# First rounds of an attention stage in a new order: second pair of keys loaded ahead of v, loads dealt out over the rounds

## The chip, the cores and the metric

The kernel runs on one core of a Trainium2 chip. The metric is the device time of one execution in microseconds (us); the median of three runs counts. A core has five engines with instruction queues of their own, each worked off in order: PE (TensorE, matrix products), DVE (VectorE), ACT (ScalarE), POOL (GpSimd) and SP (SyncE, which here only issues DMAs). PEld is PE's loading of stationary operands.

## The reference

Three stages in float32, one behind the other:

```python
# q, k, v: (2, 8, 576, 64)
q_d, k_d, v_d = means of q, k, v over 4 neighbouring positions        # 144 of them
out_d   = softmax(q_d k_d' / 8) v_d, each row repeated 4 times
out_loc = softmax(q k' / 8 where |i - j| < 4) v                       # a narrow band
x = out_d + out_loc                                                    # 1152 tokens x 512
h = x @ w_in;  x = (h * clip(h + 3, 0, 6) / 6) @ w_out                 # 512 -> 2048 -> 512
out = sum over 4 experts of p[e] * (relu(x @ w1[e]) @ w2[e])           # 512 -> 1024 -> 512
```

## The kernel before

Dense products are made in three passes over a high and a low part of each operand, so every weight is first converted (split in two) on ACT and DVE: the generator `converting()` takes one step whenever `convert(n)` asks for n of them. Six steps make one weight block (the first two blocks are called wt[0] and wt[1] here): ACT's top half (L221), DVE's L245, L255, L267 with L276, ACT's L229, and DVE's L234, which ends it.

The attention stage is the first tenth of the time. It works on eight **units** (a batch and a pair of heads; 0 to 3 are batch 0), one a round, in a loop over t (L1111 to L1176). A unit's steps on PE, with the line that the profile shows:

- `pooled_scores` (L726): scores of the pooled rows. It needs `sums`: sums over four positions of q and k, made on POOL (L450; of k on DVE, L636, in units 0 and 1) from what DMA has brought.
- `masks` and `scores` (L650, L663): the band's scores, over a mask.
- `turn` (L710) and `pooled_turn` (L780): transposes of the two softmaxes, after DVE, ACT and POOL have made them (`less_max`, `normalise`, `pooled_softmax`, `pooled_normalise`).
- `values` (L800, L811): products with v. ACT then copies the pooled part (pd, L819), DVE adds both (xf, L825), ACT and DVE split the sum (L833, L841). A unit is turned one round after its scores, its values come a round later.
- `idle_products` (L603): products of zeros whose result nobody reads.

Once per batch v is pooled: `pool_v` (L470, on PE) for batch 0; for batch 1 `pool_last_v` (L483, on PE, from v's last block of 67 rows) and `add_four(0)`, `add_four(1)` (L450 on DVE, from two loads of 512 KB that `load_four` issues at L500).

All engines but SP run in the order of the program text. PE's results go to three double banks in turn (`banks()`; a fourth, `banks(True)`, serves pool_v and values), so a step also waits until the step three banks back has been read. DMAs go through SP's queue; a load that must not start early is preceded by `hold`, a write of one element on DVE (L189), which SP waits for. The list `later` holds such loads; `load_next` takes the next one at three places of a round:

```python
    later = [
        lambda: load_half(0, 0),        # w_in, half a block
        lambda: load_half(0, 1),
        lambda: load_v(1, 0, (0,)),
        ...
        last_v,
        lambda: load_k(NU // 2 - 1, held=True),
        lambda: load_q(NU // 2 - 1, held=True),
        lambda: load_four(0),
        lambda: load_four(1),
        ...
```

From t = 8 on, `pieces(1)` puts the first products with w_in between the last units: the first (0, 0) needs wt[0], the third (0, 2) wt[1].

Of the kernel before, what the change touches and what calls it, by code (L numbers as in the profile page):

```python
# [25 lines left out]
ALU = mybir.AluOpType  # L26
AX = mybir.AxisListType
PSUM = bass.MemoryType.PSUM

P = 128  # L30
# [4 lines left out]
FACTOR = 4  # L35
# [80 lines left out]


IDLE = 11


def r32(ap):
# [4 lines left out]
def model(ctx: ExitStack, tc: tile.TileContext, qT, kT, v, dp, w_in, w_out, w1, w2, out):  # L126
# [284 lines left out]
    def load_qk(pair, at=0, n=2):  # L411
        load_k(pair, at, n)
        load_q(pair, at, n)
# [11 lines left out]
    def load_v(b, p, parts=(0, 1)):  # L425
        if 0 in parts:
            v_slots.setdefault(b, []).append(take())
        slot, o = v_slots[b][p][0], FACTOR - 1
        if b and p < 2:
            hold(slot[:, 2 * DM * parts[0] :])  # L430
        if p == 0:
            if 0 in parts:
                nc.vector.memset(slot[:o, :DM], 0.0)
                v_rows(b, p, o, 0, WR, 0, 1)
                v_rows(b, p, WP, WP - o, WP, 0, 1)
                v_rows(b, p, 0, QB - o, P, 1, 2)
# [16 lines left out]

        return v_slots[b][NP - 1][0][: KR[b][kc], (2 + kc) * DM : (3 + kc) * DM]

    def pool_v(idle):

        pool = banks(True)
        idle_products(pool, idle)
# [17 lines left out]
        for kc in range(2):  # L477
            nc.scalar.activation(out=pooled_v(0, kc), in_=pool[: KR[0][kc], kc, :], func=AF.Copy)
# [42 lines left out]
    nc.vector.memset(zeros, 0.0)  # L521
    load_qk(0, 0, 1)
    load_qk(0, 1, 1)
    for p in range(NP):
        load_v(0, p)
    load_qk(1)
    identb = const.tile([P, P], BF16, name="identb")
    make_identity(nc, identb)

# [68 lines left out]
            )  # L598
        nc.gpsimd.tensor_copy(fours[WP:], fours[:WP])

    def idle_products(ps, count):
        for n in range(count):
            nc.tensor.matmul(ps[:, n % 2, :], zeros[:, :P], zeros, start=True, stop=True)  # L603

    class Unit:
        def __init__(self, u):
# [1 line left out]
            self.b, self.hp = divmod(u, NHP)  # L608
            self.kr = KR[self.b]

        def sums(self):
# [8 lines left out]
            room = slice(2 * SK + 2 * PK, 2 * SK + 4 * PK)  # L620
            kr = KR[0]
            wide = slice(room.start, room.start + 4 * kr[0])
            own = self.k[:, FACTOR - 1 : FACTOR - 1 + S]
            k4 = k[:, base + FACTOR - 1 : base + FACTOR - 1 + NI * QT]
            k4 = k4.rearrange("p (a r j f) -> p r a j f", a=NI, r=2, f=FACTOR)
            k2 = k[:, wide].rearrange("p (a r j f) -> p r a j f", a=NI, r=2, f=2)
            if self.u >= 2:
                of = own.rearrange("p (j f) -> p j f", f=FACTOR)
                half = k[:, room].rearrange("p (j f) -> p j f", f=2)
                add(nc.gpsimd, half, of[:, :, 0:2], of[:, :, 2:4])  # L630
            if self.b:
                add(nc.gpsimd, self.kd, half[:, :, 0], half[:, :, 1])
            for r in range(0 if self.b else 2):
                to = self.kd[:, r * kr[0] : r * kr[0] + kr[r]].rearrange("p (a j) -> p a j", a=NI - r)
                if self.u < 2:
                    nc.vector.tensor_reduce(out=to, in_=k4[:, r, : NI - r], op=ALU.add, axis=AX.X)  # L636
                else:
                    two = k2[:, r, : NI - r]
                    add(nc.gpsimd, to, two[:, :, :, 0], two[:, :, :, 1])
            of = self.q.rearrange("p (j f) -> p j f", f=FACTOR)  # L640
            half = q[:, room].rearrange("p (j f) -> p j f", f=2)
            add(nc.gpsimd, half, of[:, :, 0:2], of[:, :, 2:4])
            add(nc.gpsimd, self.qd, half[:, :, 0], half[:, :, 1])

        def masks(self, idle):

# [50 lines left out]
                out=ex, in0=ex, in1=rec.unsqueeze(3).to_broadcast([QT, 2, NI, W]), op=ALU.mult  # L697
            )

        def turn(self, idle):  # L700

            tr = banks()
            idle_products(tr, idle)

            for p in range(NP):
                for h in range(2):
# [13 lines left out]
        def pooled_scores(self, idle):  # L720
            self.sd = banks()
            idle_products(self.sd, idle)
# [362 lines left out]
    def last_v():  # L1085
        load_v(1, 1, (1,))
        load_v(1, 2)

    later = [
        lambda: load_half(0, 0),  # L1090
        lambda: load_half(0, 1),
        lambda: load_v(1, 0, (0,)),
        lambda: load_v(1, 0, (1,)),
        lambda: load_v(1, 1, (0,)),
        last_v,
        lambda: load_k(NU // 2 - 1, held=True),
        lambda: load_q(NU // 2 - 1, held=True),
        lambda: load_four(0),
        lambda: load_four(1),
        lambda: load_half(1, 0),  # L1100
        lambda: load_half(1, 1),
        lambda: None,
        lambda: load_half(2, 0),
        lambda: None,
        lambda: load_half(2, 1),
    ]

    def load_next(t):
        if t > 1 and later:
            later.pop(0)()  # L1110

    make_fours()
# [1 line left out]
    for t in range(NU + 2):  # L1114
# [4 lines left out]
            )  # L1119
        if t < NU:  # L1120
            n = units[t]
            if t == 0:
                n.masks(IDLE)
                n.scores()
                n.pooled_scores(0)
                n.less_max()
                units[1].sums()
                n.pooled_softmax()
                n.normalise()
            else:  # L1130
                n.pooled_scores(4)
                n.masks(0)
                n.scores()
                n.pooled_softmax()
                if t == 1:
                    units[0].pooled_normalise()
                    make_last_fours()
                    units[2].sums()
                    load_qk(2)
                load_next(t)  # L1140
                n.less_max()
        if t == NHP + 1:
            pool_last_v()
        if t == NHP + 2:
            add_four(1)
        if 2 < t < NU + 1:
            units[t - 3].low()
        if 0 < t < NU:
            n.pooled_normalise()
            n.normalise()  # L1150
            load_next(t)
        if 0 < t < NU - 2:
            units[t + 2].sums()
        if t == NU:
            pieces(1, banks()[:, 0, :TC])
        if t >= NU:
            units[t - 2].values()
        if t > NU:
            pieces(1)
            units[t - 3].low()  # L1160
            units[t - 2].low()
        if 1 <= t <= NU:
            units[t - 1].turn(0 if t in (1, NU) else 4)
        if 2 <= t < NU:
            units[t - 2].values()
        if t == 1:
            pool_v(8)
        if 1 <= t <= NU:
            units[t - 1].pooled_turn()
        if t == NHP + 1:  # L1170
            add_four(0)
        convert(3 if t >= NU else 2 if t == 3 else 1 if t > 3 else 0)
        load_next(t)
        if t >= NU:
            pieces(1)
    attention.close()  # L1176
# [218 lines left out]
```

## Time and profile before

| | us |
|---|---|
| median of 3 runs | 654.06 (653.36 to 658.13) |
| the profiled execution | 652.78 |
| its span in the trace | 650.6 |
| PE busy | 641.2 (99% of the span) |
| DVE, ACT, POOL busy | 419.8, 252.8, 95.7 |

Between the span and the profiled execution's own time lie 2.2 us; the median is 1.28 us above that execution. PE's busy time contains the products of zeros, so in the attention stage it says little. Times below are microseconds from the start of the span.

### The profile page before, as it was taken

The numbers are of one execution on the slowest core, as the hardware profiler recorded it, in microseconds if no ns is written. First come the engines' busy times: TensorE is split into PE (matmuls) and PEld (weight loads), VectorE is DVE, ScalarE is ACT, GpSimd is POOL, SyncE is SP. The second block draws the span as 40 slices with busy tenths as digits, with TensorE's granted clock in tenths as the row PEclk, the third lists the DMA queues.
The fourth block names the chain that finished last, engine by engine and source line by source line (L and its number), as shares of the span: only waits on it lengthen the run. The fifth ranks groups of instructions, "written<-read, shape, count | busy, mean of one in ns | idle before, by whom it ended". The sixth has DMA issues, their size and how long they took to land.

```text
span 650.6 us, 11922 instructions
## 1 busy us (share of the span) xinstructions
PE 641.2 (99%) x4895; PEld 581.6 (89%) x4909; DVE 419.8 (65%) x848; ACT 252.8 (39%) x590; POOL 95.7 (15%) x141
## 2 busy tenths in 40 slices
PE   8999999999999999999999999999999999999997
PEld 3556999999999999998898998998998998988986
DVE  6579899962596238595575665665665765765742
ACT  5566666542464236352233233233241341331310
POOL 4744100000000034101201201201201201201000
PEclk9988999999999999999999999999999999999999
DMA  8764524400330110300110110120110210300012
GB/s 273 232 198 125 192 85 141 177 0 1 130 130 0 65 65 1 130 2 1 65 65 0 66 65 0 65 65 2 64 65 1 87 44 1 129 1 1 2 49 97
DMA packets 13350, 46.97 MB, mean 72 GB/s; under 512 B 1367, under 2 KB 4439, under 8 KB 9584
## 3 DMA queue, kind: packets, MB, share of 16 engines
q1 hardware_dynamic: 13296, 46.21, 20.9%
q8 instruction: 38, 0.62, 0.4%
q14 instruction: 16, 0.13, 0.1%
HBM read 43.85 MB, written 2.36 MB: 71 GB/s over the span
## 4 chain that ended last, share of the span: by engine, by line
PE 93%; DMA 3%; DVE 1%; SPq 1%; issue 0%; POOL 0%; ACT 0%; DVEq 0%; ACTq 0%; POOLq 0%
PE bank L992 27%; PE bank L382 10%; PE bank L383 10%; PE bank L384 10%; PE bank L1271 10%; PE bank L1272 10%; PE bank L1273 10%; DMA slot<-in_v_dram 2%; PE pair L800 1%; DMA slot<-in_qT_dram 1%; PE pair L603 1%; PE pair L811 1%; PE pair L780 0%; PE pair L710 0%; PE pair L726 0%
## 5 line engine op out<-in xcount | busy, mean ns | idle before, releaser
L992 PEld LDWEIGHTS bank<-xop,slot 128*128 128x128 f32 x1344 | 180.0, 188 | 1.2
L992 PE MATMUL bank<-xop,slot 128*128 128x288 f32 x1344 | 180.8, 295 | 0.0
L1272 PE MATMUL bank<-slot,h 128*128 128x512 f32 x288 | 112.2, 390 | 0.0
L1271 PE MATMUL bank<-slot,h 128*128 128x512 f32 x288 | 112.1, 389 | 0.0
L1273 PE MATMUL bank<-slot,h 128*128 128x512 f32 x288 | 112.1, 389 | 0.0
L1279 DVE SCALAR_TENSOR_TENSOR slot<-bank,pr,slot 128x512 f32<-128x512 f32 x63 | 47.3, 751 | 80.7 <-PE bank L1273 80.7
L450 POOL TENSOR_TENSOR st<-slot 128x256 f32<-128x256 f32 x16 | 13.8, 863 | 461.7 <-DMA slot<-in_w_dram 231.4
L384 PE MATMUL bank<-h,slot 128*128 128x384 f32 x192 | 64.7, 337 | 0.0
L382 PE MATMUL bank<-h,slot 128*128 128x384 f32 x192 | 64.7, 337 | 0.0
L383 PE MATMUL bank<-h,slot 128*128 128x384 f32 x192 | 64.7, 337 | 0.0
L1273 PEld LDWEIGHTS bank<-slot,h 128*128 128x128 f32 x288 | 54.1, 188 | 11.4
L1271 PEld LDWEIGHTS bank<-slot,h 128*128 128x128 f32 x288 | 54.1, 188 | 10.7
L1272 PEld LDWEIGHTS bank<-slot,h 128*128 128x128 f32 x288 | 54.1, 188 | 10.6
L382 PE MATMUL bank<-x,slot 128*128 128x384 f32 x188 | 63.2, 336 | 0.0
L384 PE MATMUL bank<-x,slot 128*128 128x384 f32 x188 | 63.0, 335 | 0.0
L383 PE MATMUL bank<-x,slot 128*128 128x384 f32 x188 | 63.0, 335 | 0.0
L450 DVE TENSOR_TENSOR u<-bank,u 128x288 f32<-128x288 f32 x96 | 43.5, 453 | 20.4 <-PE bank L992 20.0
L1021 ACT ACTIVATE h<-c 128x288 fp32r<-128x288 f32 x64 | 27.7, 445 | 71.1 <-DVE c L450 71.1
L312 ACT ACTIVATE slot<-st 128x512 fp32r<-128x512 f32 x32 | 19.2, 625 | 63.0 <-POOL st L306 63.0
L881 DVE TENSOR_TENSOR h<-slot,h 128x384 fp32r<-128x384 f32 x48 | 27.5, 586 | 24.1 <-ACT h L880 24.0
L872 ACT ACTIVATE t<-bank,half__145 128x384 f32<-128x384 f32 x47 | 27.0, 580 | 38.7 <-PE bank L384 38.4
L873 DVE SCALAR_TENSOR_TENSOR slot<-t,bank 128x384 f32<-128x384 f32 x47 | 25.7, 551 | 24.3 <-ACT t L872 24.1
(121 smaller groups left out, 925.4 us busy)
## 6 DMA issues: line engine op xcount, KB each, us to landing
slot<-in_w_dram SPq DMA_DIRECT2D x16, 1024.0 KB, 4.8
slot<-in_w_out_dram SPq DMA_DIRECT2D x8, 1024.0 KB, 4.8
slot<-in_w_in_dram SPq DMA_DIRECT2D x5, 1024.0 KB, 5.0
slot<-in_v_dram SPq DMA_DIRECT2D x8, 512.0 KB, 5.1
slot<-in_w_in_dram SPq DMA_DIRECT2D x6, 512.0 KB, 5.1
out_dram<-slot SPq DMA_DIRECT2D x9, 256.0 KB, 2.0
slot<-in_kT_dram SPq DMA_DIRECT2D x3, 576.0 KB, 7.5
slot<-in_qT_dram SPq DMA_DIRECT2D x6, 288.0 KB, 6.5
```

The source lines that it names most:

```text
L382: nc.tensor.matmul(ps, wh, xh, start=first, stop=False)
L383: nc.tensor.matmul(ps, wh, xl, start=False, stop=False)
L384: nc.tensor.matmul(ps, wl, xh, start=False, stop=last)
L450: eng.tensor_tensor(out=out, in0=a, in1=b, op=ALU.add)
L872: nc.scalar.activation(out=t, in_=ps, func=AF.Relu, bias=half_, scale=1.0 / (6.0 * UP))
L881: nc.vector.tensor_tensor(out=g[:, 1, :], in0=u, in1=r32(g[:, 0, :]), op=ALU.subtract)
L992: nc.tensor.matmul(ps, a[:, i, k], b[:, j, k], start=start and k == 0 and n == 0, stop=stop and k == 1 and n == 2, skip_group_check=True,)
L1021: nc.scalar.activation(out=self.h[:, 0, i, j], in_=of, func=AF.Relu)
L1271: nc.tensor.matmul(ps, hh, w[:, 0], start=(f == 0), stop=False)
L1272: nc.tensor.matmul(ps, hh, w[:, 1], start=False, stop=False)
L1273: nc.tensor.matmul(ps, hl, w[:, 0], start=False, stop=(f == NF - 1))
L1279: nc.vector.scalar_tensor_tensor(out=to, in0=ps, scalar=share, in1=to, op0=ALU.mult, op1=ALU.add)
```

## The change

The eight rounds are written out one by one, and steps change places in the first four:

- The loads of the second pair's keys and queries (units 2 and 3) are issued ahead of batch 0's v.
- Unit 1 is turned at the end of round 1, unit 2's scores follow at once, and `pool_v` stands in round 3 behind unit 3's pooled scores; `values` of unit 0 moves to round 3, of unit 1 to the front of round 4. Sums of k of units 2 and 3 go to DVE (L636) from POOL.
- Groups of zeros: rounds 2 and 3 have none (two groups of four each before); ahead of unit 1's turn stands one group of sixteen products of 128 columns. The other rounds keep theirs.
- Conversion starts in round 4 with two steps, where it had started in round 3 with two; the last rounds take 4 and 3 steps where they took 3 and 3.
- The list `later` is reordered and is taken from round 1 on: pair 2's loads are held, one group of loads per round differs.
- v's last block of 67 rows is loaded as 64 and 3 rows. `pool_last_v` moves from round 5 to round 6, behind unit 6's scores.

```diff
-            v_rows(b, p, 0, at, LAST_ROWS if b else WR, 0, 1)
+            v_rows(b, p, 0, at, WP if b else WR, 0, 1)
+            if b:
+                v_rows(b, p, WP, at + WP, LAST_ROWS - WP, 0, 1)
...
     load_qk(0, 1, 1)
+    load_qk(1)
     for p in range(NP):
         load_v(0, p)
-    load_qk(1)
...
     later = [
+        lambda: load_k(2, held=True),
+        lambda: load_q(2, held=True),
+        lambda: None,
+        lambda: load_v(1, 0, (0,)),
         lambda: load_half(0, 0),
         lambda: load_half(0, 1),
-        lambda: load_v(1, 0, (0,)),
         lambda: load_v(1, 0, (1,)),
+        lambda: load_k(3, held=True),
+        lambda: load_q(3, held=True),
         lambda: load_v(1, 1, (0,)),
         last_v,
-        lambda: load_k(NU // 2 - 1, held=True),
-        lambda: load_q(NU // 2 - 1, held=True),
         lambda: load_four(0),
         lambda: load_four(1),
...
+        elif t == 1:
+            n.pooled_scores(4)
+            n.masks(0)
+            n.scores()
...
+            units[2].sums_k()
+            units[3].sums_k()
+            units[3].sums_q()
+            load_next()
+            make_last_fours()
+            units[0].turn(0)
+            idle_products(banks(True), 8)
+            units[0].pooled_turn()
+            n.turn(4, SHORT_ZEROS)
+        elif t == 2:
+            n.masks(0)
+            n.scores()
+            n.pooled_scores(0)
+            n.less_max()
+            n.pooled_softmax()
+            load_next()
+            n.normalise()
+            n.pooled_normalise()
+            load_next()
+            units[1].pooled_turn()
+        elif t == 3:
+            n.pooled_scores(0)
+            pool_v()
+            n.masks(0)
+            n.scores()
...
+            units[0].values()
+            units[2].turn(0)
+            units[2].pooled_turn()
...
+        elif t < NU:
+            n.pooled_scores(4)
+            if t == NHP:
+                n.pooled_softmax()
+                load_next()
+                units[1].values()
+            n.masks(0)
+            n.scores()
+            if t == NHP + 2:
+                pool_last_v()
+            if t > NHP:
                 n.pooled_softmax()
+            load_next()
+            n.less_max()
+            if t == NHP + 2:
+                add_four(1)
+            units[0 if t == NHP else t - 3].low()
             n.pooled_normalise()
             n.normalise()
+            load_next()
...
+            units[t - 1].turn(4)
+            units[t - 2].values()
...
+            units[t - 1].pooled_turn()
+            if t == NHP + 1:
+                add_four(0)
+            convert(2 if t == NHP else 1)
+            load_next()
```

On SP's queue, behind the loads of units 0 and 1, there stood before (v is `in_v_dram`; the second pair is the k load of 128x2x576 and the first two q loads behind it):

```order
L409 DMA slot<-in_qT_dram 128x288 x2
L418 DMA slot<-in_v_dram 48x512
L418 DMA slot<-in_v_dram 64x512
L418 DMA slot<-in_v_dram 128x512
L418 DMA slot<-in_v_dram 128x2x512 x3
L418 DMA slot<-in_v_dram 48x512
L418 DMA slot<-in_v_dram 32x512
L418 DMA slot<-in_v_dram 3x512
L399 DMA slot<-in_kT_dram 128x2x576
L409 DMA slot<-in_qT_dram 128x2x288 x4
```

and now, at the same place:

```order
L411 DMA slot<-in_qT_dram 128x288 x2
L401 DMA slot<-in_kT_dram 128x2x576
L411 DMA slot<-in_qT_dram 128x2x288 x2
L420 DMA slot<-in_v_dram 48x512
L420 DMA slot<-in_v_dram 64x512
L420 DMA slot<-in_v_dram 128x512
L420 DMA slot<-in_v_dram 128x2x512 x3
```

The second pair's three loads have changed places with v's nine.

The second place is DVE's queue around `add_four`. Before, slot_890 takes the two loads, and their holds stood at the end of round 4 and in the front of round 5:

```order
L189 MEMSET slot_890 1x1
L739 TENSOR_REDUCE mxd_941<-pair_893 72x4
L741 TENSOR_SCALAR nm_943<-mxd_941 72x4
L189 MEMSET slot_890 1x1
L680 TENSOR_REDUCE mx_953<-pair_902 128x10
```

while the first use of slot_890 stood 14 rows behind the first hold, at the end of round 5 (slot_971 is another load's):

```order
L189 MEMSET slot_971 1x1
L825 TENSOR_TENSOR xf_1039<-pair_996,pd_1037 128x5x64
L825 TENSOR_TENSOR xf_1039<-pair_996,pd_1037 128x4x64
L450 TENSOR_TENSOR slot_890<-slot_890 128x2x256
L450 TENSOR_TENSOR slot_720<-slot_890 128x256
L267 TENSOR_SCALAR slot_714<-slot_714 128x1024
```

Now the slot is slot_963; the first hold stands two rows ahead of the first use, and a step of the conversion has come behind it:

```order
L191 MEMSET slot_963 1x1
L839 TENSOR_TENSOR xf_1031<-pair_988,pd_1029 128x5x64
L839 TENSOR_TENSOR xf_1031<-pair_988,pd_1029 128x4x64
L454 TENSOR_TENSOR slot_963<-slot_963 128x2x256
L454 TENSOR_TENSOR slot_942<-slot_963 128x256
L257 SCALAR_TENSOR_TENSOR slot_875<-slot_570,slot_875 128x512 x2
```

and the second hold, which follows at once, stands five rows ahead of the second use (in round 6):

```order
L191 MEMSET slot_963 1x1
L753 TENSOR_REDUCE mxd_1104<-pair_1053 72x4
L755 TENSOR_SCALAR nm_1106<-mxd_1104 72x4
L191 MEMSET slot_1114 1x1
L694 TENSOR_REDUCE mx_1117<-pair_1062 128x10
L695 TENSOR_TENSOR ex0_124<-pair_1062,mx_1117 128x2x5x38
L454 TENSOR_TENSOR slot_963<-slot_963 128x2x256
```

Both holds have moved down DVE's queue towards the two uses, which stand where they stood.

## Rows read from the trace of the kernel before

**Rows 1.** Windows: busy us and instructions of each engine, clock, DMA, just behind attention.

```profile
65.00:70.00 5.00, 5.00 (x109) 4.31 (x108) 3.44 (x7) 2.43 (x7) 1.77 (x2) 1.00 0.09 34
```

**Rows 2.** Chain of waits in order of time, to 80 us: start, us, what.

```profile
11.18 7.24 DMA slot<-in_qT_dram
...
35.38 9.11 DMA slot<-in_v_dram
```

**Rows 3.** Timeline of PE, round 1: start, us, line, tiles, count, idle before.

```profile
11.96 1.90 PE L603 MATMUL pair<-zeros 128*128 128x512 bf16 x7
...
15.21 2.79 PE L470 MATMUL pair<-slot,fours 38*16 38x512 f32 x28 [0.36 <-DMA slot<-in_v_dram]
```

**Rows 4.** Timeline of PE, round 2.

```profile
19.78 0.71 PE L726 MATMUL pair<-slot 64*72 64x144 f32 x8 [0.29 <-POOL slot L450]
20.43 0.34 PE L650 MATMUL pair<-mask,identb 128*128 128x190 bf16 x2
20.70 0.85 PE L663 MATMUL pair<-slot 64*32 64x38 f32 x72
21.47 1.04 PE L603 MATMUL pair<-zeros 128*128 128x512 bf16 x3
22.44 0.58 PE L710 MATMUL pair<-ident,ex 64*128 64x64 f32 x10
22.95 1.35 PE L800 MATMUL pair<-aT,slot 38*64 38x32 f32 x72
24.24 0.86 PE L811 MATMUL pair<-aTd,slot 80*64 80x144 f32 x8
25.03 0.70 PE L780 MATMUL pair<-ident,exd 72*80 72x72 f32 x8
25.56 1.03 PE L603 MATMUL pair<-zeros 128*128 128x512 bf16 x3
```

**Rows 5.** Groups of PEld by shape, 18 to 31 us: busy us, mean ns, idle before.

```profile
L603 PEld LDWEIGHTS <-zeros 128*128 128x128 bf16 x16 | 1.3, 97 | 1.1
```

**Rows 6.** Timeline of PE, rounds 3 to 4 and 6.

```profile
31.81 0.85 PE L811 MATMUL pair<-aTd,slot 80*64 80x144 f32 x7 [0.50 <-issue]
...
33.26 0.63 PE L603 MATMUL pair<-zeros 128*128 128x512 bf16 x1
...
35.10 1.24 PE L726 MATMUL pair<-slot 64*72 64x144 f32 x8
...
56.48 0.85 PE L780 MATMUL pair<-ident,exd 72*128 72x72 f32 x8 [0.51 <-DVE ex L681]
```

**Rows 7.** Windows, half a microsecond in round 3; the third number from the end is PE's clock.

```profile
33.00:33.50 0.50, 0.50 (x6) 0.41 (x4) 0.41 (x1) 0.06 (x1) 0.42 (x2) 0.50 0.38 94
```

**Rows 8.** Timeline of DVE, rounds 4 to 6.

```profile
42.15 1.28 DVE L255 SCALAR_TENSOR_TENSOR slot<-slot 128x512 f32<-128x512 uint32 x2
...
43.49 0.06 DVE L189 MEMSET slot<- 1x1 f32 x1
...
49.63 0.82 DVE L825 TENSOR_TENSOR xf<-pair,pd 128x320 f32<-128x320 f32 x2 [2.22 <-ACT pd L819]
...
50.37 1.57 DVE L450 TENSOR_TENSOR slot<-slot 128x512 f32<-128x512 f32 x2
...
54.35 0.74 DVE L739 TENSOR_REDUCE mxd<-pair 72x4 f32<-72x576 f32 x1
...
56.25 1.14 DVE L450 TENSOR_TENSOR slot<-slot 128x512 f32<-128x512 f32 x2
```

**Rows 9.** Line L500's own view: from DMA issue to landing, its two loads together.

```profile
DMA to landing us min/median/max: 4.8/5.1/5.4
```

**Rows 10.** DMA issues, 49 to 60 us: halves of w_in, each alone; KB, median us to landing.

```profile
slot<-in_w_in_dram SPq DMA_DIRECT2D x2, 512.0 KB, 3.5
```

**Rows 11.** Timeline of DVE and PE around wt[1]'s last step and its first use.

```profile
74.62 1.29 DVE L234 TENSOR_TENSOR slot<-slot 128x512 fp32r<-128x512 f32 x2 [0.76 <-ACT slot L229]
...
75.07 0.45 PE L382 MATMUL bank<-x,slot 128*128 128x384 f32 x1
```

More of the change, by code (lines that the diff above doesn't have):

```diff
@@ L454, in pooled_v, with pool_v @@
         return v_slots[b][NP - 1][0][: KR[b][kc], (2 + kc) * DM : (3 + kc) * DM]
-    def pool_v(idle):
+    def pool_v():
         pool = banks(True)
-        idle_products(pool, idle)
         for m in range(4):
@@ L599, in make_fours, with idle_products @@
         nc.gpsimd.tensor_copy(fours[WP:], fours[:WP])
-    def idle_products(ps, count):
-        for n in range(count):
-            nc.tensor.matmul(ps[:, n % 2, :], zeros[:, :P], zeros, start=True, stop=True)
+    def idle_products(ps, count, parts=1):
+        n = 512 // parts
+        for i in range(count * parts):
+            nc.tensor.matmul(
+                ps[:, i % 2, :n], zeros[:, :P], zeros[:, :n], start=True, stop=True
+            )
+    ROOM = slice(2 * SK + 2 * PK, 2 * SK + 4 * PK)
     class Unit:
@@ L609, in __init__, with slots @@
             self.kr = KR[self.b]
-        def sums(self):
+        def slots(self):
             pair, o = divmod(self.u, 2)
@@ L619, in sums, with sums_k @@
             self.qd = q[:, 2 * SK + o * PK : 2 * SK + (o + 1) * PK]
[L620 to L623, printed above, removed]
+            return k, q, base
+        def sums_k(self):
+            k, _, base = self.slots()
+            of = self.k[:, FACTOR - 1 : FACTOR - 1 + S].rearrange("p (j f) -> p j f", f=FACTOR)
+            if self.b:
+                self.fold(self.kd, k, of)
+                return
@@ L633, in sums @@
[L633 to L641, printed above, removed]
@@ L642, in sums, with fold @@
-            add(nc.gpsimd, half, of[:, :, 0:2], of[:, :, 2:4])
-            add(nc.gpsimd, self.qd, half[:, :, 0], half[:, :, 1])
+            for r, n in enumerate(self.kr):
+                to = self.kd[:, r * self.kr[0] : r * self.kr[0] + n]
+                nc.vector.tensor_reduce(
+                    out=to.rearrange("p (a j) -> p a j", a=NI - r),
+                    in_=k4[:, r, : NI - r],
+                    op=ALU.add,
+                    axis=AX.X,
+                )
+        def fold(self, to, slot, of):
+            half = slot[:, ROOM].rearrange("p (j f) -> p j f", f=2)
+            add(nc.gpsimd, half, of[:, :, 0:2], of[:, :, 2:4])
+            add(nc.gpsimd, to, half[:, :, 0], half[:, :, 1])
@@ L645, in masks, with sums_q, sums @@
+        def sums_q(self):
+            _, q, _ = self.slots()
+            self.fold(self.qd, q, self.q.rearrange("p (j f) -> p j f", f=FACTOR))
+        def sums(self):
+            self.sums_k()
+            self.sums_q()
         def masks(self, idle):
@@ L698, in normalise, with turn @@
             )
-        def turn(self, idle):
+        def turn(self, idle, parts=1):
             tr = banks()
-            idle_products(tr, idle)
+            idle_products(tr, idle, parts)
             for p in range(NP):
@@ L718, in turn, with pooled_scores @@
             nc.scalar.activation(out=self.aT[:, n:], in_=tr[:, 1, : n - 2 * HQ], func=AF.Copy)
-        def pooled_scores(self, idle):
+        def pooled_scores(self, idle, parts=1):
             self.sd = banks()
-            idle_products(self.sd, idle)
+            idle_products(self.sd, idle, parts)
             for qh in range(2):
@@ L1101, in model, with load_next @@
         lambda: load_half(1, 1),
-        lambda: None,
         lambda: load_half(2, 0),
-        lambda: None,
         lambda: load_half(2, 1),
     ]
-    def load_next(t):
-        if t > 1 and later:
+    def load_next():
+        if later:
             later.pop(0)()
@@ L1121, in model @@
             n = units[t]
[L1122 to L1127, printed above, removed]
-                n.pooled_softmax()
[L1129 to L1133, printed above, removed]
-                n.pooled_softmax()
[L1135 to L1141, printed above, removed]
@@ L1149, in model @@
             n.pooled_normalise()
             n.normalise()
[L1151 to L1154, printed above, removed]
+            load_next()
+            if t < NU - 2:
+                units[t + 2].sums()
+            units[t - 1].turn(4)
+            units[t - 2].values()
+            if t == NHP:
+                units[1].low()
+            units[t - 1].pooled_turn()
+            if t == NHP + 1:
+                add_four(0)
+            convert(2 if t == NHP else 1)
@@ L1155, in model @@
+            load_next()
+        elif t == NU:
+            units[t - 3].low()
             pieces(1, banks()[:, 0, :TC])
-        if t >= NU:
             units[t - 2].values()
-        if t > NU:
+            units[t - 1].turn(0)
+            units[t - 1].pooled_turn()
+            convert(4)
+        else:
+            units[t - 2].values()
             pieces(1)
@@ L1161, in model @@
             units[t - 2].low()
[L1162 to L1173, printed above, removed]
+            convert(3)
         if t >= NU:
```

35 lines of the change are left out of this document (21 added, 14 removed).

## Prediction

> **What bounds the kernel now.** I read the windows first. From 65 us on PE is busy without a gap, 5.00 of every 5.00 us at full clock [rows 1], and the change touches nothing behind the first products with w_in. So only what attention takes before that can be won or lost. PE's busy time doesn't say what bounds there, since zeros count as work; the chain of waits and the timelines do. The chain shows two transfers at its start and middle: the second pair's queries, over at 11.18 + 7.24 = 18.42 us, and v's last block, which takes 9.11 us [rows 2]. [...] Last the end of the stage: wt[1]'s final step begins at 74.62 on DVE and PE takes up its first use at 75.07 [rows 11], so there PE and DVE arrive together. A gain must hold on both engines up to that point.
>
> **What the rounds give.** All that PE does up to the end of unit 0's turn, 11.96 us [rows 3], stands in the same order, so I count from there to the values of unit 3. Durations are distances of starts in round 2 [rows 4]: pooled scores 0.65, masks 0.27, scores 0.77, four zeros 0.97, turn 0.51, values 1.29 + 0.79 = 2.08, pooled turn 0.53. Eight zeros take 1.9 [rows 3]. Pool_v's 28 last products took 2.79 [rows 3], so all 36 take 3.6. The sixteen short products of zeros are not in the trace: their columns are those of four long ones, 0.97, and sixteen weight loads of 97 ns [rows 5] would be 1.55; I take 1.3, between them, since loads overlap products in part.
>
> - Round 1: 1.9 + 0.53 + 1.3 + 0.51 = 4.2. Round 2, without zeros: 0.27 + 0.77 + 0.65 + 0.53 = 2.2.
> - Round 3: 0.65 + 3.6 + 1.04 + 2.08 + 0.51 + 0.53 = 8.4, and 0.4 for two waits for a bank (pooled scores behind DVE's subtraction, values behind ACT's copies of pool_v).
> - Round 4, with two values: 0.97 + 0.65 + 2.08 + 1.04 + 0.97 + 0.51 + 2.08 + 0.53 = 8.8. Round 5 to the end of its values: 0.97 + 0.65 + 1.04 + 0.97 + 0.51 + 2.08 = 6.2.
>
> The sum is 30.2, so unit 3's values end at 42.2; DVE's xf for them follows some 0.5 later, at 42.7, where it stood at 49.63 [rows 8]. **The lead there is 6.9 us.** [...] What hides the rest: the second pair now lands ahead of v; all those bytes together had landed by 18.42 [rows 2], and PE comes to pool_v at 11.96 + 4.2 + 2.2 + 0.2 + 0.65 = 19.2, so v is 0.8 early. The four sums of k that DVE takes over stand where it waits for unit 2's scores. Pair 2's loads go out when DVE reaches their holds, in rounds 1 and 2 (16 to 18.5 by the sum), and are wanted behind round 4's zeros, at 28.1; that covers the longest landing of such loads here. V's last block as 64 and 3 rows needs no long transfer; pool_last_v stands in round 6, where, as follows, PE has time.
>
> **What is given back.** Both loads for add_four were issued early before: the first hold stood at 43.49, the use at 50.37 [rows 8], nearly seven microseconds apart. Now the hold stands right ahead of xf, and DVE's in-order queue comes to add_four 0.74 later (49.63 to 50.37), with the transfer just issued. Everything behind it on DVE stops: a conversion step, unit 6's pooled maxima, its subtraction; and so ACT's exponentials, the pooled turn that PE does at the end of round 6, and the banks that these free. The second hold follows, and its use stands 1.9 behind it (54.35 to 56.25 [rows 8]). The price is the transfer's time. These loads took 4.8 and 5.4, but two together [rows 9]; a lone load of the same size took 3.5 [rows 10], from longer rows. I take 4.2, in the middle, and 0.1 from hold to issue:
>
> - first stop 4.2 + 0.1 - 0.74 = 3.6 (2.9 to 4.8); second 4.2 + 0.1 - 1.9 = 2.4 (1.7 to 3.6);
> - the conversion is a step later, so 1.28 of it (L255 [rows 8]) comes to lie behind xf too.
>
> Together 7.3 (5.9 to 9.7) on DVE, up to wt[1]. DVE had some idle time in there, 0.76 ahead of the last step alone [rows 11]; I let 0.5 of the delay vanish in it. PE, ahead of DVE, waits for it at three places: unit 5's pooled turn, unit 6's turn (its bank is read by ACT behind xf), and the first product with w_in, whose wt[0] is now finished one round later, at the very end of round 7. So nearly all of 6.9 is lost again: 6.9 + 0.5 - 7.3 = 0.1 ahead.
>
> [...]
>
> **The clock.** Four zeros and pooled scores behind a fall took 35.10 - 33.26 = 1.84 and 1.24, against 0.97 and 0.71 at full clock [rows 4, 6]: a fall costs 1.4. Before each fall PE had stood for 0.5 [rows 6]. Rounds 2 and 3 now have stalls of 0.2 only, but no zeros between. Between no fall (0) and one (1.4) I take 0.7, having no row that decides. Falls behind the new stops are hidden for the most part by the next wait.
>
> **Sum.** Against the profiled execution, 652.78 - 0.1 + 0.7 = 653.4; its median stood 1.28 higher, so 654.7. That is no change: 1%, 6.5 us, is about what a measurement of this kernel can tell from none.
>
> **Rivals.**
>
> - *The lead is kept.* If PE doesn't in fact wait for what stands behind add_four, only the conversion step's 1.28 is lost: 654.1 - 6.9 + 1.3 = 648.5, or 647 without the early losses of bank waits and short zeros. For it: the first stop alone meets PE late, since PE has 7 us of its own work in round 6. Against: wt[1] is just in time already [rows 11]. Chance 0.14, of which 0.06 goes beyond 1%.
> - *Slower, by the clock and slow loads.* At their long ends the stops cost 9.7; two falls in rounds 2 to 4 cost 2.8, and one behind the second stop 1.4 where PE is late: 654.1 - 6.9 + 9.7 + 2.8 + 1.4 = 661. It decides from loads of 5.4 on, with both early falls. For it: both falls of before came with half a microsecond's stall [rows 6]. Against: fewer loads are in flight now. Chance 0.07.
> - *The clock falls early.* Rounds 2 and 3 let PE's clock drop once or twice where I count half a fall: 0.7 or 2.1 more, 655.4 or 656.8, the rest as forecast. For it: both falls of before; against: these stalls are shorter. Chance 0.20. [...]
> - *The new load order does not do what it says.* If v, behind the second pair, comes later than 19.2, PE stands in round 3 and all that follows shifts: at 21 it is 2 more, 656.7. Chance 0.05.
>
> **How the numbers follow.** The forecast's case has 0.54 and holds 651.5 to 657; early falls and a late v (0.25) lie at its upper end. The range runs from 649.5 to 660, into the kept lead below and the slow case above, and leaves some 0.15 out. Faster by over 1% needs the lead whole (0.06), slower by over 1% the long ends together (0.07); the same 0.87.
>
> **What would show it.** DVE's xf for unit 3 at about 42.7; behind it an idle stretch of 3 to 5 us on DVE ahead of the first add_four and one of 2 to 3.5 ahead of the second, both put down to the DMA of v; PE idle for about 2 us ahead of unit 5's pooled turn and again ahead of unit 6's turn; the third pass of the first product with w_in waiting for L236 (the old L234). The forecast is wrong if those loads land within two microseconds, if DVE's stops are there and PE still arrives at wt[1] early, or if PE's clock is at 0.50 for more than one stretch ahead of 42 us.

## The result and the profile after

The changed kernel takes 659.33 us (median of 11 runs, 656.81 to 661.46); the kernel before, run beside it, 654.54 (11 runs, 652.92 to 660.62). The ratio is 1.0055 with a 95% interval of 1.0035 to 1.0076: half a per cent slower, inside the one per cent that was forecast as no change. The profiled execution took 659.33, its span is 657.4, and its mean granted clock 0.982, where the kernel before had 0.995.

The first rounds, in PE's timeline of the kernel after (start, us, line, tiles, count, idle before; zeros are L607 now, the turn L724, pooled scores L740, values L814):

```profile
11.91 0.56 PE L724 MATMUL pair<-ident,ex 64*128 64x64 f32 x10 [0.75 <-POOL ex L710]
12.41 1.90 PE L607 MATMUL pair<-zeros 128*128 128x512 bf16 x8
...
14.65 1.00 PE L607 MATMUL pair<-zeros 128*128 128x128 bf16 x15
16.59 0.23 PE L607 MATMUL pair<-zeros 128*128 128x128 bf16 x1 [0.94 <-issue]
...
35.23 1.23 PE L814 MATMUL pair<-aT,slot 38*64 38x32 f32 x62 [0.31 <-issue]
...
38.13 1.91 PE L607 MATMUL pair<-zeros 128*128 128x512 bf16 x4
```

Unit 0's turn waits 0.75 for POOL, and the zeros behind it begin at 12.41, 0.45 later than the 11.96 from which the sum counts [rows 3]. Of that, 0.34 stood already at unit 1's pooled scores (9.41, in the kernel before 9.07), and conv_early below, the same program up to here, begins these zeros at 11.45: executions differ by as much. The short zeros stall for 0.94 ahead of the last; values stall for 0.31 in round 4; and at 38.13 four zeros take 1.91, from start to start 1.85 for the 0.97 of [rows 4], with the clock at 0.50 from 37.3 to 40.5.

DVE's timeline around the two uses of `add_four` (now L454; xf is L839, the hold L191), which answers to [rows 8]:

```profile
45.52 0.06 DVE L191 MEMSET slot<- 1x1 f32 x1
46.23 0.82 DVE L839 TENSOR_TENSOR xf<-pair,pd 128x320 f32<-128x320 f32 x2 [0.65 <-ACT pd L833]
50.72 1.15 DVE L454 TENSOR_TENSOR slot<-slot 128x512 f32<-128x512 f32 x2 [3.67 <-DMA slot<-in_v_dram]
51.79 1.28 DVE L257 SCALAR_TENSOR_TENSOR slot<-slot 128x512 f32<-128x512 uint32 x2
...
53.02 0.06 DVE L191 MEMSET slot<- 1x1 f32 x1
...
57.15 1.15 DVE L454 TENSOR_TENSOR slot<-slot 128x512 f32<-128x512 f32 x2 [2.14 <-DMA slot<-in_v_dram]
```

Unit 3's xf stands at 46.23, 3.4 ahead of [rows 8]; then both loads are waited for. Their times, in the chain of waits (start, us, what):

```profile
45.63 5.00 DMA slot<-in_v_dram
...
53.11 4.01 DMA slot<-in_v_dram
```

And what PE makes of it, in its timeline again (L794 is the pooled turn, L825 the pooled part of values, L384 a first pass with w_in):

```profile
55.15 1.19 PE L794 MATMUL pair<-ident,exd 72*128 72x72 f32 x8 [1.61 <-DVE ex L695]
56.14 1.91 PE L607 MATMUL pair<-zeros 128*128 128x512 bf16 x4
...
62.17 1.87 PE L607 MATMUL pair<-zeros 128*128 128x512 bf16 x4 [1.52 <-ACT aTd L802]
...
64.80 2.34 PE L814 MATMUL pair<-aT,slot 38*64 38x32 f32 x72
...
73.90 1.75 PE L814 MATMUL pair<-aT,slot 38*64 38x32 f32 x72
...
77.41 0.42 PE L384 MATMUL bank<-x,slot 128*128 128x384 f32 x1
...
79.67 1.35 PE L814 MATMUL pair<-aT,slot 38*64 38x32 f32 x72
...
81.74 0.45 PE L384 MATMUL bank<-x,slot 128*128 128x384 f32 x1
```

The windows of those stretches (busy us and instructions of PE, PEld, DVE, ACT, POOL; the third number from the end is the clock):

```profile
54.00:62.00 8.00, 5.50 (x94) 3.43 (x95) 5.55 (x14) 3.92 (x15) 1.93 (x2) 0.52 0.47 152
62.00:74.50 12.50, 12.31 (x138) 9.03 (x139) 7.30 (x18) 7.14 (x21) 1.93 (x2) 0.50 0.31 115
74.50:82.00 7.50, 7.50 (x179) 6.31 (x175) 5.52 (x12) 4.66 (x12) 0.00 (x0) 0.98 0.19 44
```

From 54.4 to 74.5 us the clock is at 0.50, with PE busy for 12.31 of the last 12.50. From the zeros at 62.17 to the second values at 73.90 PE needs 11.73. At full clock the same work is 0.97 + 0.51 + 2.08 + 0.53 [rows 4] and 2.26 for a product with w_in (77.41 to 79.67 above), 6.35 together. So the clock adds 5.4 to PE's work behind the second wait. That is the most it can have cost: at full clock PE would have come to the first product with w_in some 3 us sooner, and could have met the conversion step L236 there, for which late_use below waits 1.82. The third product with w_in begins at 81.74, where before it stood at 75.07 [rows 11]: 6.7 later, which is the whole difference of the spans (657.4 - 650.6 = 6.8).

**Theory.** The late holds stop DVE and through it PE; behind PE's two waits the clock stays at 0.50, and that, more than the waits, is what the prediction left out. **Rivals:** the conversion step that came later sets the end; the missing zeros alone let the clock fall; or the stalls named "issue" do.

### The profile page after: what moved, and what is told of

Its sections match the earlier page's. It is cut to its first block, busy times and chain, and to the rows that moved or that the text cites. A ratio compares the mean times of both kernels' runs of the same rounds, so it can differ in the third digit from the quotient of the medians.

```text
span 657.4 us, 11944 instructions
## 1 busy us (share of the span) xinstructions
PE 646.5 (98%) x4909; PEld 586.5 (89%) x4909; DVE 419.0 (64%) x854; ACT 253.5 (39%) x590; POOL 92.5 (14%) x135
## 4 chain that ended last, share of the span: by engine, by line
PE 95%; DVE 2%; DMA 1%; issue 1%; ACT 0%; POOL 0%; DVEq 0%; POOLq 0%
PE bank L1006 27%; PE bank L384 10%; PE bank L386 10%; PE bank L385 10%; PE bank L1334 10%; PE bank L1333 10%; PE bank L1335 10%; PE pair L607 2%; PE pair L814 1%; DMA slot<-in_v_dram 1%; PE pair L825 1%; PE pair L794 1%; PE pair L473 1%; PE pair L724 1%; PE pair L677 0%
## 5 line engine op out<-in xcount | busy, mean ns | idle before, releaser
L454 POOL TENSOR_TENSOR st<-slot 128x256 f32<-128x256 f32 x16 | 13.8, 863 | 466.9 <-DVE slot L319 205.1
L384 PE MATMUL bank<-h,slot 128*128 128x384 f32 x192 | 64.7, 337 | 0.0
L384 PE MATMUL bank<-x,slot 128*128 128x384 f32 x188 | 63.2, 336 | 0.0
L454 DVE TENSOR_TENSOR u<-bank,u 128x288 f32<-128x288 f32 x96 | 43.5, 453 | 20.2 <-PE bank L1006 19.8
L886 ACT ACTIVATE t<-bank,half__145 128x384 f32<-128x384 f32 x47 | 27.1, 580 | 37.4 <-PE bank L386 37.3
L887 DVE SCALAR_TENSOR_TENSOR slot<-t,bank 128x384 f32<-128x384 f32 x47 | 25.7, 551 | 23.6 <-ACT t L886 23.4
```

Source lines behind the costliest of these rows:

```text
L384: nc.tensor.matmul(ps, wh, xh, start=first, stop=False)
L454: eng.tensor_tensor(out=out, in0=a, in1=b, op=ALU.add)
L886: nc.scalar.activation(out=t, in_=ps, func=AF.Relu, bias=half_, scale=1.0 / (6.0 * UP))
```

## The experiments

Ratios are to the kernel before, run on the same chip beside each; "clock" is the mean over the runs of each run's granted clock (0.990 to 0.993 for the kernel before).

| kernel | median us | ratio, 95% interval | clock |
|---|---|---|---|
| late_use | 654.27 | 0.9983 (0.9957 to 1.0009) | 0.990 |
| before_late_holds | 657.82 | 1.0047 (1.0025 to 1.0069) | 0.990 |
| long_zeros | 662.58 | 1.0081 (1.0044 to 1.0117) | 0.977 |
| zeros_23 | 662.16 | 1.0101 (1.0062 to 1.0140) | 0.983 |
| late_use_conv | 655.39 | 0.9988 (0.9964 to 1.0013) | 0.988 |
| late_use_conv2 | 655.36 | 1.0004 (0.9978 to 1.0031) | 0.988 |
| conv_early | 658.63 | 1.0047 (1.0019 to 1.0076) | 0.984 |
| before_split | 651.96 | 0.9933 (0.9908 to 0.9958) | 0.999 |
| late_use_conv3 | 651.44 | 0.9948 (0.9925 to 0.9970) | 0.993 |
| spread_zeros | 651.46 | 0.9937 (0.9918 to 0.9957) | 0.994 |
| split_late_holds | 660.43 | 1.0078 (1.0052 to 1.0105) | 0.986 |
| spread_gate | 650.08 | 0.9902 (0.9870 to 0.9933) | 0.996 |

**late_use**, the changed kernel with both uses a round later:

```diff
             if t == NHP + 2:
+                add_four(0)
+            if t == NHP + 3:
                 add_four(1)
...
-            if t == NHP + 1:
-                add_four(0)
```

> The changed kernel with both uses of add_four one round later on DVE (the first where the second stood, the second behind unit 7's subtraction); the holds and loads stay. Late holds, with the clock behind them (my theory): the stops of 3.67 and 2.14 us on DVE are gone, so are PE's two waits of 1.61 and 1.52 and the stretch of 20 us at a clock of 0.50. The trace of the changed kernel was 3.4 ahead at unit 3's xf and 6.7 behind at the third piece with w_in, so 10.1 were lost in between; all of it but the 1.3 of the later conversion step comes back: 659.3 - 8.8 = 650.5, with falls of 3.4 us at most. Late holds alone, the clock independent of them: the half clock stays, 5.8 come back at most: 653.5. Conversion late (rival): wt[0] and wt[1] hold PE anyway, at most 1 comes back: 658 to 659, and DVE's wait moves to the first products with w_in.

Measured: 654.27, five below the changed kernel (ratios 1.0055 and 0.9983, intervals apart). DVE doesn't stop at `add_four` any more, as its timeline shows, and PE's two waits are gone:

```profile
50.76 1.14 DVE L454 TENSOR_TENSOR slot<-slot 128x512 f32<-128x512 f32 x2
```

So the late holds are a cause, by about 5. But 8.8 were expected, and neither theory had the rest right: PE came to the first product with w_in at 60.93 and met there the wait for the conversion that the rival had named, in its timeline:

```profile
60.93 0.42 PE L384 MATMUL pair<-x,slot 128*128 128x384 f32 x1
61.19 0.34 PE L385 MATMUL pair<-x,slot 128*128 128x384 f32 x1
63.35 0.69 PE L386 MATMUL pair<-x,slot 128*128 128x384 f32 x1 [1.82 <-DVE slot L236]
```

and behind that wait the clock, in a window, was at 0.50 for 13 us with PE busy for 12.15 of them:

```profile
62.50:75.50 13.00, 12.15 (x118) 10.77 (x119) 6.98 (x14) 6.57 (x16) 0.25 (x1) 0.50 0.08 11
```

**before_late_holds**, the kernel before with only the two holds and loads moved down (`load_four` itself, not shown, no longer takes the slot):

```diff
-        lambda: load_four(0),
-        lambda: load_four(1),
-        lambda: load_half(1, 0),
-        lambda: load_half(1, 1),
+        lambda: four_slots.append(take()),
+        lambda: None,
+        lambda: (load_four(0), load_half(1, 0)),
+        lambda: (load_four(1), load_half(1, 1)),
```

> The kernel before with only the two holds and loads for add_four issued later, the first just ahead of unit 3's xf, the second behind the conversion step of round 5; slots, PE's order and conversion as before. Late holds with the clock: stops on DVE of 3.5 to 4.5 and 2 to 3, two waits of PE, a stretch of some 20 us at 0.50; nothing hides it, since wt[1] was just in time: 654.5 + 8 to 10 = 662 to 664. Late holds alone: 654.5 + 5 to 6 = 660. Conversion late (rival): the conversion stands where it stood, so within 2 of the kernel before: 654.5 to 656.5.

Measured: 657.82, below both forms of the theory (660, and 662 to 664) and above the rival (654.5 to 656.5). Its trace shows why it decides little: only the second stop came (1.74). PE had waited 2.34 at `pool_last_v`, and the clock then lay at 0.50 from 45.5 to 55, so that xf came late and the first load was there. PE's timeline there:

```profile
44.66 1.03 PE L483 MATMUL pair<-slot,last_fours 67*16 67x512 f32 x2 [2.34 <-DVE recd L764]
```

and the window behind it:

```profile
45.50:55.00 9.50, 9.50 (x109) 5.66 (x110) 2.54 (x6) 2.91 (x7) 6.13 (x10) 0.50 0.37 116
```

The wait is put down to DVE's work for a softmax that `pool_last_v` doesn't use, so it was another's, most likely the load of v's last block, for which this place waited before (0.47 put down to DMA). That load took 9.11 in the kernel before [rows 2]; its 64 rows alone, in the changed kernel, took 4.9 from issue to landing. before_split and split_late_holds below take it away.

**long_zeros** (`n.turn(4)` for `n.turn(4, SHORT_ZEROS)`: four long zeros for the sixteen short ones):

> The changed kernel with four products of zeros of 512 columns ahead of unit 1's turn in place of sixteen of 128. Short zeros cost (theory): the sixteen took 1.00 and a stall of 0.94 ahead of the last, 2.1 to the turn, four long ones take 0.97; unit 1's turn comes 1.1 earlier and so does unit 3's xf; the holds move with it, so the end does too: 658.2. The stall belongs to a place in PE's instructions and not to the short products (rival): it turns up elsewhere in the first rounds, xf gains 0.2 at most: 659.

Measured: 662.58, where 658.2 or 659 was expected, with an interval that overlaps that of the changed kernel; in its profile unit 3's xf stood at 52.12, later and not earlier, and the mean clock of that execution (665.52) was 0.969. The stall at the short zeros was gone, but one of 0.49 stood in round 3. As a test of the time it is inconclusive; as a hint at what the stalls are it was worth most, see below.

**zeros_23**, the changed kernel with three groups of four zeros back:

```diff
             n.scores()
-            n.pooled_scores(0)
+            n.pooled_scores(4)
...
         elif t == 3:
-            n.pooled_scores(0)
+            n.pooled_scores(4)
...
-            units[2].turn(0)
+            units[2].turn(4)
```

> The changed kernel with three groups of four zeros back in rounds 2 and 3 (ahead of both pooled scores and of unit 2's turn), 0.97 each. Missing zeros let the clock fall at 37.2 (theory C): the fall is gone, 2.9 paid and 1.4 given back, unit 3's xf 1.5 later: 660.8. The fall comes from the stall of 0.31 at 34.92 (rival): it is still there, some 3 us later, xf 2.9 later: 662.2.

Measured: 662.16 (four runs, 659.44 to 664.63), as the rival had it. The falls are still there, from 39 and from 49 us on (four zeros take 1.91 at 39.59 and at 49.80), and so are the stalls. Missing zeros as such are not it, which is as far as this run goes.

**What the stalls are.** In each trace I counted PE's matmuls up to the stall: a window from 0 to it, in which the count stands behind PE's busy time. Of the changed kernel, up to its second stall:

```profile
0.00:35.20 35.20, 31.31 (x727) 18.79 (x727) 22.19 (x71) 20.33 (x68) 19.58 (x51) 1.00 0.76 234
```

Of long_zeros, the window up to its first:

```profile
0.00:25.33 25.33, 22.15 (x473) 11.96 (x473) 17.51 (x55) 14.98 (x51) 15.47 (x43) 1.00 0.81 249
```

and PE's timeline there, which shows how far the 72 products of unit 0's values had come:

```profile
23.96 0.89 PE L814 MATMUL pair<-aT,slot 38*64 38x32 f32 x46 [0.15 <-ACT slot L481]
25.34 0.66 PE L814 MATMUL pair<-aT,slot 38*64 38x32 f32 x26 [0.49 <-issue]
```

Of late_use, the window up to its second:

```profile
0.00:25.13 25.13, 21.39 (x473) 12.48 (x473) 17.02 (x55) 14.84 (x50) 15.43 (x43) 1.00 0.82 251
```

with PE's timeline there:

```profile
23.90 0.77 PE L814 MATMUL pair<-aT,slot 38*64 38x32 f32 x34 [0.15 <-ACT slot L481]
25.14 0.88 PE L814 MATMUL pair<-aT,slot 38*64 38x32 f32 x38 [0.47 <-issue]
```

And of zeros_23, the window up to its longest, of 1.66 us:

```profile
0.00:48.15 48.15, 42.75 (x984) 25.35 (x984) 30.52 (x93) 26.65 (x87) 25.35 (x59) 0.96 0.71 215
```

Over the kernels they lie behind 220 (ahead of the sixteenth short product), 473, 727 and 984 matmuls, 253 to 257 apart, whatever stands there: with twelve zeros fewer, the stall at 473 comes twelve values later (46 of 72 for 34 of 72). No kernel stalls at all four (the changed one at 220 and 727), and the stall of the kernel before at 31.81 [rows 6] lies behind 603 weight loads, one and a half steps behind 220. The page of the changed kernel, in its part on DMA queues (packets, MB, share of 16 engines), has 38 transfers of instructions on one queue, 16 KB each:

```profile
q8 instruction: 38, 0.62, 0.4%
```

PE's 4909 matmuls and 4909 weight loads in that run, divided by 38, are 258 for one, an estimate that counts all 38 as PE's; a step of 254 matmuls with their loads is about two of them. Narrow windows of the DMA view tell when such a transfer starts: at 13.9 and 32.8 us in the changed kernel and at 45.6 in zeros_23. PE goes on at 16.59, 35.23 and 48.16, which is 2.4 to 2.7 later, after stalls as different as 0.94, 0.31 and 1.66. Over the twenty stalls named "issue" of 0.2 and more in the traces it is 2.4 to 2.8 (gaps among zeros of which a record is missing are left out). So I read the stalls, of 0.2 to 1.66, as PE running out of instructions until a transfer has come. That is an inference from the counts and these starts: no view says which engine a transfer is for. That short products, which use up the instructions of a transfer sooner, are the reason is tested by spread_zeros.

**conv_early, late_use_conv, late_use_conv2 and late_use_conv3** move wt[0]'s last step. The first two, on the changed kernel and on late_use:

```diff
             units[t - 1].turn(4)
+            if t == NU - 1:
+                convert(1)
             units[t - 2].values()
...
-            convert(2 if t == NHP else 1)
+            if t < NU - 1:
+                convert(2 if t == NHP else 1)
```

late_use_conv2 also has `convert(2)` ahead of round 8's `pieces(1, ...)` and two, for four, at its end; late_use_conv3 has the first `convert(1)` behind `n.less_max()` instead.

> The changed kernel with nothing but the last step of wt[0] taken ahead of unit 5's values in round 7; the late holds stay. Late holds with the clock (theory): PE, at half clock, came to the third pass of the first product behind L236 (ended 70.95 against a product begun at 69.6); at most 1.3 comes back: 658 to 659.3. Conversion late (rival): wt[0] is what holds PE at the end; 3 or more come back: 656.

> late_use with the last step of wt[0] (L236) taken ahead of unit 5's values in round 7, in place of behind them; so it stands ahead of xf on DVE. Next wait (my theory after late_use): with the stops gone PE reached the first product with w_in at 60.9 and waited 1.82 us for that step, and the clock stood at 0.50 for 13 us behind that wait. Now the wait is under 0.3 and that stretch is gone or 3.4 long: 654.3 - 1.8 - some 2 of the clock = 650.5. Clock by itself (rival): falls come from stalls in the first rounds as often as before; only the 1.8 come back, or less, since wt[1] comes next: 652.5 to 654.

> late_use_conv, and two of the four conversion steps of round 8 ahead of the first product with w_in (on DVE ahead of unit 6's xf, where it was idle for 3.07 and 2.78 us in late_use). If wt[1] is the next bound at the third product (theory: PE and DVE came together there in the kernel before [rows 11], and now PE is some 4 ahead): 1 to 2 below late_use_conv, 649. If the clock holds PE back there and not DVE (rival): the same as late_use_conv within 0.7.

> late_use_conv2 with the last step of wt[0] (L236) taken directly behind unit 7's subtraction, ahead of add_four(1). In late_use_conv and late_use_conv2 that step began at 62.2 and 60.2, behind unit 7's sums, took 2.56 us beside POOL's two products in place of 1.29, and PE waited 1.93 and 2.48 for it. Now it stands ahead of them: PE's wait is under 0.3 and the fall behind it is gone. wt[0] as the next wait (theory): 655.3 - 2 to 3 = 652.5 to 653.3, with what the clock loses in rounds 3 to 5 left over. The waits cost nothing, the clock falls all the same (rival): 655.

Measured: conv_early 658.63, not told apart from the changed kernel; with the late holds in, conversion is not what sets the end. late_use_conv and late_use_conv2 gave nothing (655.4 both), against my expectation for the first. The step had moved, but it was not done sooner. DVE's timeline has the step, in late_use_conv:

```profile
62.19 2.56 DVE L236 TENSOR_TENSOR slot<-slot 128x512 fp32r<-128x512 f32 x2
```

and in late_use_conv3:

```profile
57.34 1.28 DVE L236 TENSOR_TENSOR slot<-slot 128x512 fp32r<-128x512 f32 x2
```

In late_use_conv POOL's products ran from 61.67 to 63.60 beside it, in late_use_conv3 POOL stood still. There PE doesn't wait for the step, and the time is 651.44, four less. The two traces show 2.56 beside POOL and 1.28 without it; that POOL is the reason is my reading, and no run tests it alone.

**before_split**, the kernel before with v's last block as 64 and 3 rows:

```diff
-            v_rows(b, p, 0, at, LAST_ROWS if b else WR, 0, 1)
+            v_rows(b, p, 0, at, WP if b else WR, 0, 1)
+            if b:
+                v_rows(b, p, WP, at + WP, LAST_ROWS - WP, 0, 1)
```

> The kernel before with v's last block as 64 and 3 rows and nothing else. The 67-row load was over at 35.38 + 9.11 [rows 2] and pool_last_v, which waited 0.47 for it, now doesn't: the load takes some 4 us, PE's wait is gone; 0.5 to 1.5 below the kernel before if the path runs through it (with a fall of the clock less), 654; if wt[1] sets the end all the same (rival): no change, 655.3.

Measured: 651.96, 0.67% faster than the kernel before, more than either theory. PE no longer waits at `pool_last_v`, in its timeline:

```profile
44.55 1.02 PE L485 MATMUL pair<-slot,last_fours 67*16 67x512 f32 x2
```

The mean clock is 0.999, and four of its five runs lie at or below 652.1, where the runs of the kernel before begin. So this one part of the change is a gain. That the saved wait of half a microsecond is worth three through the clock is argued from before_late_holds's trace, where a longer wait at the same place (2.34) had a clock of 0.50 for 9.5 us behind it. The profiled executions of the two kernels don't show it: their spans are 650.6 and 650.4.

**split_late_holds**, before_split with the edit of before_late_holds:

> before_split with the two holds and loads for add_four issued late, as in before_late_holds; the wait for v's last block (2.34 us in that kernel's trace, with a fall of 10 us behind it, which delayed xf and so hid the first stop) is not there. Late holds (theory): stops on DVE of 3 to 4 and 2 to 2.5, a wait of PE at unit 5's pooled turn and a fall of the clock behind it: 652.0 + 5 to 8 = 657 to 660. Late holds are harmless without the change's other parts (rival): within 1.5 of before_split, 652 to 653.5.

Measured: 660.43, 8.5 above before_split (by the ratios, which allow for the different chips, 1.45%) and a little above what the theory expected. Now the mechanism stands without the change's other parts, the split rows apart. DVE's timeline has the two stops:

```profile
50.82 1.15 DVE L452 TENSOR_TENSOR slot<-slot 128x512 f32<-128x512 f32 x2 [2.20 <-DMA slot<-in_v_dram]
...
58.42 1.15 DVE L452 TENSOR_TENSOR slot<-slot 128x512 f32<-128x512 f32 x2 [2.86 <-DMA slot<-in_v_dram]
```

PE's timeline has the wait behind them:

```profile
63.44 0.59 PE L603 MATMUL pair<-zeros 128*128 128x512 bf16 x1 [4.50 <-ACT aTd L788]
```

and the window there the clock:

```profile
62.00:75.00 13.00, 11.34 (x121) 8.77 (x125) 7.59 (x17) 6.63 (x21) 2.61 (x3) 0.50 0.26 82
```

**spread_zeros**, late_use_conv3 with zeros where PE's products are short:

```diff
-            n.turn(4, SHORT_ZEROS)
+            n.turn(4)
...
             pool_v()
-            n.masks(0)
+            n.masks(4)
...
                 units[1].values()
-            n.masks(0)
+            n.masks(4 if t == NHP else 0)
```

> late_use_conv3 with the sixteen short zeros as four long ones, and four zeros more ahead of unit 3's masks (behind pool_v) and ahead of unit 4's masks (between two values and scores). PE's stalls in the first rounds lie in every kernel so far behind the same counts of matmuls, 220, 473, 727 and 983, 253 to 256 apart, wherever in the program that falls; so I put them down to PE's instructions, which come in blocks and come late where short products follow one another. Blocks of instructions (theory): with more long products in rounds 1, 3 and 4 a block lasts longer, the stalls shrink below 0.3 each, the clock keeps above 0.993; 1.94 paid, 0.9 saved at the short zeros, 2 to 4 given back: 650.5 to 652 where late_use_conv3 has 653. Clock falls by the lack of zeros are no matter (rival): stalls and falls stay, it is 1 slower: 654.

Measured: 651.46, the same as late_use_conv3, with a mean clock of 0.994 for 0.993: what the eight added zeros cost came back, and no more. In its profiled execution (658.86) no stall named "issue" of 0.2 or more stands between 12 and 49 us, where late_use_conv3 has 0.88 at 15.50 and 0.84 at 34.88, and none does in the next kernel's. With the longer products these stalls are thus gone, as the theory had it; that this makes the kernel faster is not shown.

**spread_gate**, spread_zeros with round 8's first `convert(2)` behind `pieces(1, ...)`:

> spread_zeros with the two early conversion steps of round 8 directly behind the first product with w_in instead of ahead of it. In late_use_conv3 unit 7's pooled turn waited 1.53 us for the bank that L887 reads, since L247 and L257 (1.9 together) stood ahead of L887 on DVE, and the clock fell behind that wait. Now L887 stands ahead of them: no such wait, no fall there; wt[1] ends some 1 later than there, still ahead of the third product. The wait is what is left of PE's stalls from round 7 on (theory): the mean clock is 0.996 or above and the time 649.5 to 650.5, against 651.5. DVE becomes the bound instead, wt[1] too late (rival): PE waits for L236 at the third product, 651.5 to 652.5.

Measured: 650.08, ratio 0.9902: a version that beats both kernels, by 0.98% (0.67 to 1.30) for the one before. Its interval (0.9870 to 0.9933) meets that of before_split (0.9908 to 0.9958), which changes nothing but v's last block. Its windows show the clock at 1.00 from 14 to 70 us and one fall behind:

```profile
14.00:70.00 56.00, 53.44 (x1329) 35.92 (x1328) 44.24 (x114) 34.90 (x112) 25.49 (x41) 1.00 0.60 182
70.00:76.00 6.00, 6.00 (x76) 5.56 (x69) 3.78 (x7) 3.19 (x7) 0.00 (x0) 0.72 1.00 407
```

No stall named "issue" is left in PE's timeline up to 84 us, and unit 7's pooled turn no longer waits for L887, as the theory had it. The last fall follows a wait of 0.92 for ACT's copy of a turn (at 69.45).

## Why the prediction was right, and where it was not

The sum missed by some 5 us, and its range held the time. That it did is partly luck: the upper end came from the slow rival, whose conditions (loads from 5.4 on, two early falls) did not come, and what carried the time there, a long fall behind the second stop, was in no term at that size.

- **What the rounds give** came out at 3.4 for 6.9 at unit 3's xf. Rounds 2 and 3 took what was worked out (17.27 to 28.30). Lost were 0.45 up to unit 0's turn, 0.34 of it ahead of unit 1's pooled scores, which conv_early's execution did not lose; 0.8 at the short zeros, which took 2.1 with their stall for the 1.3 that I had put between two bounds; 0.31 in round 4; 1.4 for a fall of the clock; and 0.65 that xf itself waited for ACT.
- **What is given back** was right: stops of 3.67 and 2.14 for 3.6 and 2.4, loads of 5.00 and 4.01 for 4.2 each, PE idle for 1.61 and 1.52 at the two places named. The third place, the first product with w_in, didn't wait to speak of; there PE was by then too slow. By split_late_holds the late holds cost 8.5 with what follows them, by late_use some 5 in the changed kernel.
- **The clock** is the term that was mis-sized. It had 0.7, and "falls behind the new stops are hidden for the most part by the next wait". The fall behind the first stop was hidden: its slow zeros and scores (56.14 to 60.65) ended in the wait for ACT. Behind the second there was no next wait, and the half clock went on up to 74.5: up to 5.4 us, and 1.4 for the fall at 37.2, where the term had 0.7 in all. I had taken the length of a fall from [rows 6, 7]; in that trace both lasted some 3.5 us (a clock of 0.52 over 33 to 36.5 and of 0.53 over 57 to 60.5), and nothing there said that a fall ends so soon after each wait.
- **The rivals.** The clock's early fall came, at one stretch ahead of 42 us. Slower by clock and slow loads came nearest in time (661), with a load of 5.0 and one early fall instead of loads of 5.4 and two; what it counted at 1.4 behind the second stop took up to 5.4. The lead was not kept. V was not late: `pool_v` started at 20.35 without a wait.
- **Left out** was the gain in v's last block, which the prediction counted as no more than room for `pool_last_v`: 0.67% when made alone. The change's ratio of 1.0055 thus holds a part that gains and late holds that cost more. That the exchange of rounds gains anything by itself is not shown: with the late holds undone and conversion moved, late_use_conv3 (0.9948, 0.9925 to 0.9970) is no faster than before_split (0.9933), and late_use (0.9983) is if anything slower. The exchange without the split rows was not run.

What stays open: why a fall of the clock lasts 3.5 us in one run (33 to 36.5 in the kernel before, PE busy for 3.28) and 20 in another (54.4 to 74.5 in the changed one, PE busy for 17.81 of 20.10), and when it comes at all. In late_use_conv3 PE stalls for 0.88 at 15.50 and for 0.84 at 34.88, and the clock is at 1.00 from 14 to 64 us; in the changed kernel it fell at 37.2, behind a stall of 0.31. No kernel here held one thing fixed and changed that, so the clock's part in the 4.8 us that the change cost is read from the traces and not isolated; the late holds' part is shown by taking them away (late_use) and by adding them (split_late_holds).

## What to carry to other kernels

When a load is moved towards its use, look up what stands between hold and use in the in-order queue, and compare that time with the landing of a like load, here 4 to 5 us for 512 KB. A wait of PE costs more than its length where the clock falls behind it, here up to 5.4 us behind a wait of 1.52, so a stop of 2 us on another engine is priced with the slow stretch that may follow, not alone. And where short products follow one another, look for stalls named "issue" before taking longer ones out as waste: here PE stalled for up to 1.66 at such places, and putting longer ones back cost as much as it saved (651.46 for 651.44).

## What the runs showed of the hardware that was not expected

- In rounds with short products PE stalled for 0.2 to 1.66 us behind some of the counts of 220, 473, 727 and 984 matmuls, and went on 2.4 to 2.8 us after a transfer of 16 KB of instructions had started; in spread_gate's rounds it did not stall so.
- The clock stayed at 0.50 for 12.5 us in which PE was busy for 12.31 (the kernel after), and for 13 with 12.15 (late_use).
- A subtraction of DVE took 2.56 beside POOL's products (late_use_conv) and 1.28 with POOL still (late_use_conv3).
- Repeated runs of one kernel can differ by 9 us, and their clock goes with it: late_use took 650.64 in a run at 0.997 and 659.66 in one at 0.978.
